# Prologue of an attention and SwiGLU kernel: first loads through one GpSimd queue, key sums on the full array, more TensorE spins

## The chip, the cores and the metric

The kernel runs on one core of one Trainium2 chip (trn2). The metric is device time in microseconds (us) of one execution, the median over runs. Before the change it is 323.82 us, the median of 6 runs (323.05 to 325.52). Engines are named as in the profile: PE is TensorE, DVE is VectorE, ACT is ScalarE, POOL is GpSimd, SP is SyncE. SP and POOL (and ACT, twice at the end) start transfers.

## The reference

Inputs are q, k, v of shape (8, 8, 576, 64) in float32 (batch, heads, sequence, head dimension) and the weights w_gate, w_val (512 x 1536) and w_out (1536 x 512). Two stages follow each other:

```python
q_s = softmax(q, axis=-1)            # over the head dimension
k_s = softmax(k, axis=2)             # over the sequence
kv  = einsum('bhsd,bhse->bhde', k_s, v)
att = einsum('bhsd,bhde->bhse', q_s, kv)
x   = att.transpose(0, 2, 1, 3).reshape(4608, 512)
g   = x @ w_gate
out = (g * sigmoid(g) * (x @ w_val)) @ w_out     # float32, 4608 x 512
```

## The kernel before

Exponentials are taken without subtracting a maximum, and products run in bf16 with float32 sums. A batch has 576 rows, and its eight heads are two groups (G) of four. A group's tile has 128 partitions: partitions 0 to 63 carry one pair of heads (g = 0), 64 to 127 the other (g = 1), and each partition holds T = 9 rows of each head of its pair.

For one group the attention stage is: load q, k and v (`load`, L72, by SP; for batch 0 v is loaded by POOL, cast to bf16 on the way, L358); exp of q and k on ACT (`exp_of`, L119); row sums of exp(q), their reciprocal and the product on DVE (`norm_sum` L132, `norm_mul` L146); nine 128 x 128 transposes of the result on PE, in two PSUM banks of 5 and 4 (`turn_pe` L158, BANKS = (0, 5), (5, 9)), copied out by ACT or DVE (`turn_out` L170); kv, 18 matmuls with 64 contraction rows each; scaling of kv by the reciprocal of the key sums into `kn`; and `x_one` (L213), eight small matmuls whose results are copied into `xt`, the transposed input of the feed-forward stage.

The feed-forward stage works through units. `m_unit` (L278) makes 128 of the 1536 hidden columns for a chunk of tokens: matmuls with the gate weights (`g_ps`) and the value weights (`u_ps`), Silu on ACT (L297), product on DVE (L298). Batch 0 is the first chunk: 12 units, each with 16 matmuls of 320 or 256 columns. `o_unit` (L325) multiplies 128 tokens by w_out and stores. Later chunks interleave `m_unit`, `o_unit` and the attention of the next batch.

The order of instructions on each engine is the order in which the program writes them (`tc.manual_schedule()`), so the body from L344 on sets it. At the start, in before:

- SP issues q group 0 in two pieces, q group 1, k group 0, k group 1 (L345 to L348).
- POOL builds the identity (L343), then issues v group 0, which waits until k group 0 has landed (L360), v group 1, ten weight slices (L361 to L363: 128, 256, 384, 384, 384 columns of w_gate and w_val in turn) and four slices of w_out (L364). The program has eight semaphores for POOL's transfers, so a transfer waits for the eighth before it.
- ACT: exp of q 0 (two pieces), q 1, k 0, k 1, then copies and scalings.
- PE: seven spins that start with the first row sum (`spin`, L377: matmuls of a tile of zeros, whose results nobody reads), the transposes of group 0, `key_sum(0)` (L384: 18 matmuls of k's exp with a column of ones, two row groups of 64), two spins, `key_sum(1)`, one spin, `kv_first(0)` (L400), half the transposes of group 1, `x_one(0, 0)`, the other half, `kv_first(1)`, `x_one(0, 1)`, then `m_unit` 0 to 11.
- SP issues batch 1's loads when the third slice of w_out has landed (L432).

Of the kernel before, what the change touches and what calls it, by code (L numbers as in the profile page):

```python
# [8 lines left out]
FP32 = mybir.dt.float32  # L9
# [6 lines left out]
def kernel(  # L16
# [36 lines left out]
    xt = const.tile([128, KT, n_tok], BF16, name="xt", tag="xt")  # L53
    hr = const.tile([128, MT, RING], BF16, name="hr", tag="hr")
    ident = const.tile([128, 128], BF16, name="ident", tag="ident")
    ones = const.tile([128, 1], BF16, name="ones", tag="ones")
    zero = const.tile([128, 512], BF16, name="zero", tag="zero")
    vbs = [const.tile([128, T, 130], BF16, name=f"vb{i}", tag=f"vb{i}") for i in range(2)]
    v16 = [const.tile([128, 2, T * 64], BF16, name=f"v16_{i}", tag=f"v16_{i}") for i in range(2)]
# [83 lines left out]
        nc.vector.reciprocal(out=rr, in_=rs)  # L143
        return first

    def norm_mul(b, G, pieces=((0, T),)):  # L146
        s = st[b, G]
        eq2 = s["eq"].rearrange("p t h d -> p (t h) d")
        qs = s["qs"] = at.tile([128, T, 128], BF16, tag="qs", name="qs")
        for t0, t1 in pieces:  # L150
            n = 2 * (t1 - t0)
            nc.vector.tensor_mul(  # L152
                qs[:, t0:t1, :].rearrange("p t (h d) -> p (t h) d", d=64),
                eq2[:, 2 * t0:2 * t1, :],
                s["rr"][:, 2 * t0:2 * t1].to_broadcast([128, n, 64]),
            )
# [183 lines left out]

    make_identity(nc, ident)  # L343
    with tc.manual_schedule():  # L344
        load("q", q, 0, 0, BANKS)  # L345
        load("q", q, 0, 1)
        k0 = load("k", k, 0, 0)
        load("k", k, 0, 1)  # L348
        warm = const.tile([128, 1], FP32, name="warm", tag="warm")
        nc.vector.memset(warm, 0.0)  # L350
        nc.scalar.activation(out=warm, in_=warm, func=AF.Exp)
        nc.vector.memset(zero, 0.0)
        nc.vector.memset(ones, 1.0)
        for vb in vbs:
            nc.vector.memset(vb[:, :, 128:129], 1.0)

        for G in range(NG):
            d = nc.gpsimd.dma_start(out=v16[G], in_=head_ap(v, 0, G))  # L358
            if G == 0:
                tc.add_manual_dep(d.ins, k0.ins.name, SYNC, reason="order of loads")  # L360
        for c0, n in ((0, 128), (128, 256), (384, 384), (768, 384), (1152, 384)):  # L361
            w_slice(wg, moe_w_gate, c0, n)
            w_slice(wv, moe_w_val, c0, n)  # L363
        w_dma = [wo_slice(m0, 3) for m0 in (0, 3, 6, 9)]  # L364

        exp_of("q", 0, 0, BANKS)
        exp_of("q", 0, 1)
        exp_of("k", 0, 0)
        exp_of("k", 0, 1)
        first = norm_sum(0, 0, BANKS)  # L370
        norm_mul(0, 0, BANKS)
        norm_sum(0, 1)
        norm_mul(0, 1, BANKS)

        idle = bank("idle")

        def spin(n, after=None):  # L377
            for _ in range(n):
                i = nc.tensor.matmul(out=idle, lhsT=zero[:, 0:128], rhs=zero, start=True, stop=True)  # L379
                if after is not None:  # L380
                    tc.add_manual_dep(i.ins, after.ins.name, SYNC, reason="start of the warm-up")
                    after = None

        def key_sum(G):  # L384
            s = st[0, G]
            s["kv"] = [bank("kv") for _ in range(2)]
            for t in range(T):
                for g in range(2):
                    r = slice(64 * g, 64 * g + 64)
                    nc.tensor.matmul(  # L390
                        out=s["kv"][g][:, 128:129], lhsT=ek_of(0, G, g, t), rhs=ones[r, :],
                        start=(t == 0), stop=(t == T - 1),
                    )
            s["kvr"] = []
            for g in range(2):
                kvr = at.tile([128, 1], FP32, tag=f"kvr{g}", name="kvr")
                nc.vector.reciprocal(out=kvr, in_=s["kv"][g][:, 128:129])
                s["kvr"].append(kvr)

        def kv_first(G):  # L400
            s = st[0, G]
            for t in range(T):
                for g in range(2):
                    r = slice(64 * g, 64 * g + 64)
                    nc.tensor.matmul(
                        out=s["kv"][g][:, 0:128].rearrange("p (h d) -> p h d", d=64),
                        lhsT=ek_of(0, G, g, t), rhs=v16[G][r, :, 64 * t:64 * t + 64],
                        start=(t == 0), stop=(t == T - 1),
                    )
            kn = s["kn"] = at.tile([128, 2, 128], BF16, tag="kn1", name="kn1")  # L410
            nc.scalar.mul(kn[:, 0, :], s["kv"][0][:, 0:128], s["kvr"][0])
            nc.vector.tensor_scalar_mul(kn[:, 1, :], s["kv"][1][:, 0:128], s["kvr"][1])

        spin(7, first)
        turn_pe(0, 0, 0)
        turn_pe(0, 0, 1)
        key_sum(0)
        turn_out(0, 0, 0, nc.scalar)
        turn_out(0, 0, 1, nc.scalar)
        spin(2)  # L420
        key_sum(1)
        spin(1)
        kv_first(0)
        turn_pe(0, 1, 0)
        turn_out(0, 1, 0, nc.scalar)
        x_one(0, 0)
        turn_pe(0, 1, 1)
        turn_out(0, 1, 1, nc.vector)
        kv_first(1)
        x_one(0, 1)  # L430

        load_batch(1, w_dma[-2], by_group=True)  # L432
        load_batch(2)

        for m in range(MT):
            m_unit(0, S, m, by_part=(m == 0))

        for G in range(NG):
            exp_of("q", 1, G)
            exp_of("k", 1, G)  # L440
            cast_v(1, G)
        norm_sum(1, 0)
        norm_mul(1, 0)
        o_unit(0)
        o_unit(1)
        turn_pe(1, 0, 0)
        turn_pe(1, 0, 1)
        turn_out(1, 0, 0, nc.vector)
        turn_out(1, 0, 1, nc.vector)
        kv_one(1, 0)  # L450
        norm_sum(1, 1)
        scale_one(1, 0, (nc.vector, nc.vector))
        norm_mul(1, 1)
        p = o_mm(2)
        x_one(1, 0)
        turn_pe(1, 1, 0)
        turn_pe(1, 1, 1)
        o_out(2, p)
        turn_out(1, 1, 0, nc.vector)
        turn_out(1, 1, 1, nc.vector)  # L460
        kv_one(1, 1)
        scale_one(1, 1, (nc.vector, nc.vector))
        o_unit(3)
        x_one(1, 1)
        for what in ("q", "k"):
            for G in range(NG):
                exp_of(what, 2, G)

        chunks = [(S, 448)] + [(c, 512) for c in range(1024, n_tok, 512)]
        for ci, (c0, n) in enumerate(chunks):  # L470
            b = ci + 2
            jo = 4 * ci
            att = b < B
            final = ci == len(chunks) - 1
            for m in range(MT):
                if ci == 0:
                    if m == 1:
                        cast_v(b, 0)
                        cast_v(b, 1)
                        norm_sum(b, 0)  # L480
                    elif m == 2:
                        norm_mul(b, 0)
                        turn_dma(b, 0)
                    elif m == 3:
                        norm_sum(b, 1)
                    elif m == 4:
                        norm_mul(b, 1)
                        turn_dma(b, 1)
                elif m == 3:
                    if att:  # L490
                        exp_of("q", b, 0)
                        exp_of("q", b, 1)
                        norm_sum(b, 0)
                    o_unit(jo)
                    if att:
                        norm_mul(b, 0)
                        turn_dma(b, 0)
                    o_unit(jo + 1)
                    if att:
                        norm_sum(b, 1)  # L500
                elif m == 4 and att:
                    norm_mul(b, 1)
                    turn_dma(b, 1)
                elif m == 7:
                    if att:
                        exp_of("k", b, 0)
                        exp_of("k", b, 1)
                        cast_v(b, 0)
                        cast_v(b, 1)
                    o_unit(jo + 2)  # L510
                    if not final:
                        o_unit(jo + 3)
                if att and m == 8:
                    kv_both(b)
                    scale_both(b)
                    if b + 1 < B:
                        load_batch(b + 1)
                m_unit(c0, n, m)
                if att and m == 9:
                    x_both(b)  # L520
        o_unit(jo + 3)
        last = n_tok // 128 - 4
        for j in range(last, last + 3):
            o_unit(j)
        o_last(last + 3)
# [30 lines left out]
```

## Time and profile before

| what | value |
|---|---|
| median of 6 runs | 323.82 us |
| the profiled execution | 324.37 us |
| its span in the profile | 322.4 us |
| first load issued (SP) | 0.74 us |
| first exp starts (ACT) | 4.08 us |
| first spin (PE) | 5.73 us |
| first v load issued (POOL) | 9.43 us |
| first kv matmul of group 0 / group 1 | 13.57 / 16.76 us |
| first m_unit starts | 18.97 us |
| first o_unit starts | 43.65 us |

Times in the profile count from the start of its span. A row of the timeline reads: start, duration, engine, line, operation, tile written <- tiles read, shape, number of instructions, and in brackets the idle time before it and what ended that. A row of the chain of waits reads: start, duration, what. The rows of the transfers give the time from issue to landing.

### The profile page before, as it was taken

The numbers are of one execution on the slowest core, as the hardware profiler recorded it, in microseconds if no ns is written. First come the engines' busy times: TensorE is split into PE (matmuls) and PEld (weight loads), VectorE is DVE, ScalarE is ACT, GpSimd is POOL, SyncE is SP. The second block draws the span as 40 slices with busy tenths as digits, with TensorE's granted clock in tenths as the row PEclk, the third lists the DMA queues.
The fourth block names the chain that finished last, engine by engine and source line by source line (L and its number), as shares of the span: only waits on it lengthen the run. The fifth ranks groups of instructions, "written<-read, shape, count | busy, mean of one in ns | idle before, by whom it ended". The sixth has DMA issues, their size and how long they took to land.

```text
span 322.4 us, 4896 instructions
## 1 busy us (share of the span) xinstructions
PE 309.2 (96%) x1902; PEld 153.8 (48%) x1902; DVE 165.5 (51%) x282; ACT 144.3 (45%) x209; POOL 28.8 (9%) x36
## 2 busy tenths in 40 slices
PE   2899998999999999999999999999999999999995
PEld 1468754445444544444444444544444444444443
DVE  4534459388492639354835484457535333333421
ACT  3653363645547355644573467346634122302300
POOL 0850011200110020002000200011000000000000
PEclk9999999999999999999999999999999999999999
DMA  7899999627743944485438633872430112020125
GB/s 239 147 196 204 190 380 393 220 38 201 278 102 69 318 156 103 71 278 196 88 70 249 238 68 72 224 283 47 91 67 0 35 33 65 0 58 9 34 52 115
DMA packets 40360, 45.75 MB, mean 142 GB/s; under 512 B 17424, under 2 KB 24336, under 8 KB 40336
## 3 DMA queue, kind: packets, MB, share of 16 engines
q1 hardware_dynamic: 32752, 39.99, 42.3%
q0 software_dynamic: 7424, 5.31, 11.0%
q8 instruction: 15, 0.25, 0.3%
q10 hardware_dynamic: 160, 0.13, 0.2%
q14 instruction: 9, 0.07, 0.1%
HBM read 37.75 MB, written 9.44 MB: 146 GB/s over the span
## 4 chain that ended last, share of the span: by engine, by line
PE 84%; DMA 6%; DVE 4%; ACT 3%; issue 1%; SPq 0%; POOL 0%
PE g_ps L289 28%; PE u_ps L289 27%; PE o_ps L314 25%; PE kv L191 2%; DMA k<-in_k_dram 2%; DMA out_dram<-o_sb 2%; DMA v<-in_v_dram 2%; DVE rs L138 2%; PE xp L259 1%; ACT eq L124 1%; DVE qs L152 1%; PE o_ps L334 1%; ACT ek L124 1%; DVE hr L298 1%; SPq L77 0%
## 5 line engine op out<-in xcount | busy, mean ns | idle before, releaser
L297 ACT ACTIVATE sg<-g_ps 128x512 bf16<-128x512 f32 (+2 forms) x120 | 65.0, 555 | 138.2 <-PE g_ps L289 132.7
L298 DVE TENSOR_TENSOR hr<-sg,u_ps 128x512 bf16<-128x512 bf16 (+2 forms) x120 | 74.4, 630 | 90.1 <-PE u_ps L289 83.0
L289 PE MATMUL g_ps<-xt,wg 128*128 128x512 bf16 (+2 forms) x480 | 112.4, 361 | 0.3 <-ACT xt L228 0.2
L289 PE MATMUL u_ps<-xt,wv 128*128 128x512 bf16 (+2 forms) x480 | 111.2, 358 | 0.0
L314 PE MATMUL o_ps<-wo,hr 128*128 128x512 bf16 x420 | 93.6, 379 | 0.0
L289 PEld LDWEIGHTS <-wv 128*128 128x128 bf16 x480 | 47.1, 98 | 46.9 <-issue 0.4
L289 PEld LDWEIGHTS <-wg 128*128 128x128 bf16 x480 | 46.2, 99 | 45.9 <-issue 1.3
L314 PEld LDWEIGHTS <-hr 128*128 128x128 bf16 x420 | 41.0, 98 | 49.1
L322 DVE COPY o_sb<-o_ps 128x512 f32<-128x512 f32 x35 | 23.7, 681 | 40.3 <-PE o_ps L314 40.3
L127 POOL CAST vb<-v 128x1152 bf16<-128x1152 f32 x14 | 16.1, 1148 | 176.6 <-DMA v<-in_v_dram 142.7
L138 DVE TENSOR_REDUCE rs<-eq 128x18 f32<-128x1152 bf16 (+2 forms) x17 | 21.6, 1278 | 12.8 <-ACT eq L124 12.8
L152 DVE TENSOR_TENSOR qs<-eq,rr 128x1152 bf16<-128x1152 bf16 (+2 forms) x18 | 21.7, 1214 | 0.1
L124 ACT ACTIVATE eq<-q 128x1152 bf16<-128x1152 f32 (+2 forms) x17 | 18.1, 1104 | 5.1 <-DMA q<-in_q_dram 5.0
L124 ACT ACTIVATE ek<-k 128x1152 bf16<-128x1152 f32 x16 | 18.0, 1158 | 1.0 <-DMA k<-in_k_dram 1.0
L297 ACT ACT_TABLE_LOAD x12 | 15.4, 1283 | 0.2
L124 ACT ACT_TABLE_LOAD x11 | 14.1, 1283 | 0.2
L379 PE MATMUL idle<-zero 128*128 128x512 bf16 x10 | 4.8, 626 | 5.7 <-DVE rs L138 5.7
L191 PE MATMUL kv<-vb,ek 64*128 64x129 bf16 x252 | 8.9, 217 | 0.2 <-DVE hr L298 0.2
L191 PEld LDWEIGHTS <-ek 64*128 64x128 bf16 x252 | 7.4, 94 | 3.0 <-ACT sg L297 2.1
L267 ACT CAST xt<-xp 128x512 bf16<-128x512 f32 x12 | 6.4, 589 | 3.8 <-PE xp L259 3.8
L268 DVE CAST xt<-xp 128x512 bf16<-128x512 f32 x12 | 7.7, 683 | 0.0
L228 ACT CAST xt<-xp 128x320 bf16<-128x320 f32 (+1 forms) x8 | 2.8, 404 | 8.3 <-PE xp L221 8.3
(43 smaller groups left out, 70.5 us busy)
## 6 DMA issues: line engine op xcount, KB each, us to landing
k<-in_k_dram SPq DMA_DIRECT2D x16, 576.0 KB, 7.1
out_dram<-o_sb SPq DMA_DIRECT2D x70, 128.0 KB, 2.4
q<-in_q_dram SPq DMA_DIRECT2D x15, 576.0 KB, 5.1
v<-in_v_dram SPq DMA_DIRECT2D x14, 576.0 KB, 8.9
wo<-in_moe_w_out_dram POOLq DMA_DIRECT2D x4, 384.0 KB, 15.1
wg<-in_moe_w_gate_dram POOLq DMA_DIRECT2D x3, 384.0 KB, 11.3
wv<-in_moe_w_val_dram POOLq DMA_DIRECT2D x3, 384.0 KB, 11.6
v<-in_v_dram POOLq DMA_DIRECT2D x2, 288.0 KB, 5.3
```

The costliest lines, as they stand in the source:

```text
L124: nc.scalar.activation(out=e[:, t0:t1], in_=src[:, t0:t1], func=AF.Exp)
L127: nc.gpsimd.tensor_copy(out=vbs[G][:, :, 0:128].rearrange("p t (h d) -> p t h d", d=64), in_=raw["v", b, G].rearrange("p h (t d) -> p t h ...
L138: i = nc.vector.reduce_sum(out=rs[:, 2 * t0:2 * t1], in_=eq2[:, 2 * t0:2 * t1, :], axis=mybir.AxisListType.X)
L152: nc.vector.tensor_mul(qs[:, t0:t1, :].rearrange("p t (h d) -> p (t h) d", d=64), eq2[:, 2 * t0:2 * t1, :], s["rr"][:, 2 * t0:2 * t1].to_b ...
L191: nc.tensor.matmul(out=kv[g][:, c:c + 129], lhsT=ek_of(b, G, g, t), rhs=vbs[G][r, t, 0:129], start=(t == 0), stop=(t == T - 1),)
L267: nc.scalar.copy(out=xt[:, 2 * G, c0:c0 + 512], in_=main[G][0])
L268: nc.vector.tensor_copy(out=xt[:, 2 * G + 1, c0:c0 + 512], in_=main[G][1])
L289: nc.tensor.matmul(out=ps[i][:, 0:w_], lhsT=w[:, kk, ms], rhs=xt[:, kk, c:c + w_], start=(kk == 0), stop=(kk == KT - 1),)
L297: nc.scalar.activation(out=sg[:, 0:w_], in_=g_ps[:, 0:w_], func=AF.Silu)
L298: nc.vector.tensor_mul(hr[:, m, r:r + w_], sg[:, 0:w_], u_ps[:, 0:w_])
L314: nc.tensor.matmul(out=o_ps, lhsT=hr[:, m, r0:r0 + 128], rhs=wo[:, m, :], start=(m == 0), stop=(m == MT - 1),)
L322: nc.vector.tensor_copy(out=o_sb, in_=o_ps)
```

## The change

All first loads of batch 0 move from SP to POOL and stand in one queue: q 0, q 1, k 0, k 1, v 0, v 1 in two pieces, then the identity, then the weights. v no longer waits for k. q 0 is no longer split. The second half of group 0's q product is made by POOL, ahead of the weights in its queue. The key sums become 9 matmuls per group with all 128 contraction rows and a two-column selector `sel` (column g is one in the partitions of g) in place of 18 with 64 rows. exp of k 1 moves behind group 0's two copies on ACT. Both halves of group 1's transposes move ahead of `key_sum(1)` and `kv_first(0)`. The spins become 8 (from the start) + 6 (with the first row sum) + 3 + 2 + 2 + 2. `kv_first(1)` is written as two pieces, one for each piece of v 1, and the scaling becomes a function of its own. Batch 1's loads wait for the second w_out slice in place of the third.

```diff
-    ones = const.tile([128, 1], BF16, name="ones", tag="ones")
+    sel = const.tile([128, 2], BF16, name="sel", tag="sel")
...
-    def norm_mul(b, G, pieces=((0, T),)):
+    def norm_mul(b, G, pieces=((0, T),), engs=None):
...
-        for t0, t1 in pieces:
+        for (t0, t1), eng in zip(pieces, engs or (nc.vector, nc.vector)):
             n = 2 * (t1 - t0)
-            nc.vector.tensor_mul(
+            eng.tensor_mul(
...
-    make_identity(nc, ident)
     with tc.manual_schedule():
-        load("q", q, 0, 0, BANKS)
-        load("q", q, 0, 1)
-        k0 = load("k", k, 0, 0)
-        load("k", k, 0, 1)
+        for what, src in (("q", q), ("k", k)):
+            for G in range(NG):
+                t_ = raw[what, 0, G] = ld.tile([128, 2, T * 64], FP32, tag=what, name=what)
+                nc.gpsimd.dma_start(out=t_, in_=head_ap(src, 0, G))
+        nc.gpsimd.dma_start(out=v16[0], in_=head_ap(v, 0, 0))
+        for t0, t1 in BANKS:
+            nc.gpsimd.dma_start(out=v16[1][:, :, 64 * t0:64 * t1], in_=head_ap(v, 0, 1, t0, t1))
...
+        nc.vector.memset(sel, 0.0)
+        for g in range(2):
+            nc.vector.memset(sel[64 * g:64 * g + 64, g:g + 1], 1.0)
...
-        for G in range(NG):
-            d = nc.gpsimd.dma_start(out=v16[G], in_=head_ap(v, 0, G))
-            if G == 0:
-                tc.add_manual_dep(d.ins, k0.ins.name, SYNC, reason="order of loads")
+        make_identity(nc, ident)
+
+        exp_of("q", 0, 0, BANKS)
+        exp_of("q", 0, 1)
+        exp_of("k", 0, 0)
+
+        first = norm_sum(0, 0, BANKS)
+        norm_mul(0, 0, BANKS, (nc.vector, nc.gpsimd))
+        norm_sum(0, 1)
+        norm_mul(0, 1, BANKS)
+
         for c0, n in ((0, 128), (128, 256), (384, 384), (768, 384), (1152, 384)):
...
-        exp_of("q", 0, 0, BANKS)
-        exp_of("q", 0, 1)
-        exp_of("k", 0, 0)
-        exp_of("k", 0, 1)
-        first = norm_sum(0, 0, BANKS)
-        norm_mul(0, 0, BANKS)
-        norm_sum(0, 1)
-        norm_mul(0, 1, BANKS)
...
         def key_sum(G):
             s = st[0, G]
-            s["kv"] = [bank("kv") for _ in range(2)]
+            ks = bank("ks")
             for t in range(T):
-                for g in range(2):
-                    r = slice(64 * g, 64 * g + 64)
-                    nc.tensor.matmul(
-                        out=s["kv"][g][:, 128:129], lhsT=ek_of(0, G, g, t), rhs=ones[r, :],
-                        start=(t == 0), stop=(t == T - 1),
-                    )
...
+                nc.tensor.matmul(
+                    out=ks[:, 0:2], lhsT=s["ek"][:, t, :, :].rearrange("p h d -> p (h d)"), rhs=sel,
+                    start=(t == 0), stop=(t == T - 1),
+                )
+            s["kvr"] = at.tile([128, 2], FP32, tag="kvr", name="kvr")
+            nc.vector.reciprocal(out=s["kvr"], in_=ks[:, 0:2])
...
-        spin(7, first)
+        spin(8)
+        spin(6, first)
         turn_pe(0, 0, 0)
         turn_pe(0, 0, 1)
-        key_sum(0)
         turn_out(0, 0, 0, nc.scalar)
         turn_out(0, 0, 1, nc.scalar)
+        exp_of("k", 0, 1)
+        key_sum(0)
+        spin(3)
+        turn_pe(0, 1, 0)
+        turn_pe(0, 1, 1)
+        turn_out(0, 1, 0, nc.scalar)
+        turn_out(0, 1, 1, nc.vector)
+        key_sum(1)
         spin(2)
-        key_sum(1)
-        spin(1)
         kv_first(0)
-        turn_pe(0, 1, 0)
-        turn_out(0, 1, 0, nc.scalar)
+        scale_first(0)
+        spin(2)
         x_one(0, 0)
-        turn_pe(0, 1, 1)
-        turn_out(0, 1, 1, nc.vector)
-        kv_first(1)
+        kv_first(1, *BANKS[0])
+        kv_first(1, *BANKS[1])
+        scale_first(1)
+        spin(2)
         x_one(0, 1)
 
-        load_batch(1, w_dma[-2], by_group=True)
+        load_batch(1, w_dma[-3], by_group=True)
         load_batch(2)
```

More of the change, by code (lines that the diff above doesn't have):

```diff
@@ L352 @@
         nc.vector.memset(zero, 0.0)
-        nc.vector.memset(ones, 1.0)
+        nc.vector.memset(sel, 0.0)
+        for g in range(2):
+            nc.vector.memset(sel[64 * g:64 * g + 64, g:g + 1], 1.0)
         for vb in vbs:
             nc.vector.memset(vb[:, :, 128:129], 1.0)
-        for G in range(NG):
-            d = nc.gpsimd.dma_start(out=v16[G], in_=head_ap(v, 0, G))
-            if G == 0:
-                tc.add_manual_dep(d.ins, k0.ins.name, SYNC, reason="order of loads")
+        make_identity(nc, ident)
[6 more added lines that the diff above has]
+        norm_mul(0, 1, BANKS)
         for c0, n in ((0, 128), (128, 256), (384, 384), (768, 384), (1152, 384)):
@@ L364 @@
         w_dma = [wo_slice(m0, 3) for m0 in (0, 3, 6, 9)]
-        exp_of("q", 0, 0, BANKS)
-        exp_of("q", 0, 1)
-        exp_of("k", 0, 0)
-        exp_of("k", 0, 1)
-        first = norm_sum(0, 0, BANKS)
-        norm_mul(0, 0, BANKS)
-        norm_sum(0, 1)
-        norm_mul(0, 1, BANKS)
-        idle = bank("idle")
         def spin(n, after=None):
+            idle = bank("idle")
             for _ in range(n):
@@ L385, in key_sum, with kv_first @@
             s = st[0, G]
-            s["kv"] = [bank("kv") for _ in range(2)]
+            ks = bank("ks")
             for t in range(T):
-                for g in range(2):
-                    r = slice(64 * g, 64 * g + 64)
-                    nc.tensor.matmul(
-                        out=s["kv"][g][:, 128:129], lhsT=ek_of(0, G, g, t), rhs=ones[r, :],
-                        start=(t == 0), stop=(t == T - 1),
-                    )
[L394 to L400, printed above, removed]
+                nc.tensor.matmul(
[4 more added lines that the diff above has]
+            nc.vector.reciprocal(out=s["kvr"], in_=ks[:, 0:2])
+        def kv_first(G, t0=0, t1=T):
             s = st[0, G]
-            for t in range(T):
+            if t0 == 0:
+                s["kv"] = [bank("kv") for _ in range(2)]
+            for t in range(t0, t1):
                 for g in range(2):
@@ L409, in kv_first, with scale_first @@
                     )
+        def scale_first(G):
+            s = st[0, G]
             kn = s["kn"] = at.tile([128, 2, 128], BF16, tag="kn1", name="kn1")
-            nc.scalar.mul(kn[:, 0, :], s["kv"][0][:, 0:128], s["kvr"][0])
-            nc.vector.tensor_scalar_mul(kn[:, 1, :], s["kv"][1][:, 0:128], s["kvr"][1])
-        spin(7, first)
+            nc.scalar.mul(kn[:, 0, :], s["kv"][0][:, 0:128], s["kvr"][:, 0:1])
+            nc.vector.tensor_scalar_mul(kn[:, 1, :], s["kv"][1][:, 0:128], s["kvr"][:, 1:2])
+        spin(8)
+        spin(6, first)
         turn_pe(0, 0, 0)
         turn_pe(0, 0, 1)
-        key_sum(0)
         turn_out(0, 0, 0, nc.scalar)
         turn_out(0, 0, 1, nc.scalar)
+        exp_of("k", 0, 1)
[6 more added lines that the diff above has]
+        key_sum(1)
         spin(2)
-        key_sum(1)
-        spin(1)
         kv_first(0)
-        turn_pe(0, 1, 0)
-        turn_out(0, 1, 0, nc.scalar)
+        scale_first(0)
+        spin(2)
         x_one(0, 0)
-        turn_pe(0, 1, 1)
-        turn_out(0, 1, 1, nc.vector)
-        kv_first(1)
+        kv_first(1, *BANKS[0])
+        kv_first(1, *BANKS[1])
+        scale_first(1)
+        spin(2)
         x_one(0, 1)
-        load_batch(1, w_dma[-2], by_group=True)
+        load_batch(1, w_dma[-3], by_group=True)
         load_batch(2)
```

## The prediction

> **What bounds the kernel now.** I read the page's busy row first, then the chain of waits for the first 45 us, then the timeline of the same stretch engine by engine, then the landing times of the transfers.
>
> The page's first part:
>
> ```profile
> PE 309.2 (96%) x1902; PEld 153.8 (48%) x1902; DVE 165.5 (51%) x282; ACT 144.3 (45%) x209; POOL 28.8 (9%) x36
> ```
>
> TensorE (PE) is busy 309.2 of 322.4 us. The waits of PE from 60 us to the end sum to 0.4 us. So whatever moves the end of the first feed-forward unit (m_unit 0 of batch 0) moves the end of the program by the same amount, and the change touches only what lies before that point, plus the start of batch 1's loads. The chain of waits (start us, us, what):
>
> ```profile
> 2.28 6.85 DMA k<-in_k_dram
> 9.13 0.30 issue
> 9.43 0.86 POOL v L358
> 10.29 6.43 DMA v<-in_v_dram
> 16.72 0.04 issue
> 16.76 1.16 PE kv L405 x18
> 17.92 0.37 ACT kn L411
> 18.29 0.04 issue
> 18.33 0.71 PE xp L221 x8
> 19.04 2.04 PE g_ps L289 x8
> 21.08 1.18 PE u_ps L289 x8
> 22.25 0.98 PE g_ps L289 x8
> ```
>
> Two things cost time here. First, v is asked for only when k's first load has landed (9.13), so the second v load lands at 16.72. Second, m_unit 0 takes 2.04 + 1.18 = 3.22 us, every later one 0.98 + 0.98 = 1.96: TensorE still runs at half speed. The profile's granted clock says 1.00 throughout, so that column does not show this; the matmul rows do. From the timeline:
>
> ```profile
> 5.73 3.17 PE L379 MATMUL idle<-zero 128*128 128x512 bf16 x7 [5.73 <-DVE rs L138]
> ...
> 10.60 1.16 ACT L124 ACTIVATE ek<-k 128x1152 bf16<-128x1152 f32 x1 [0.28 <-DMA k<-in_k_dram]
> ...
> 13.57 1.14 PE L405 MATMUL kv<-v,ek 64*128 64x128 bf16 x18 [0.82 <-DMA v<-in_v_dram]
> ```
>
> The seven spins start 0.43 us apart (3.0 us in all, transposes follow at 8.69), against about 0.2 us for a 512-column matmul later (o_ps: 24 in 5.34). The 18 kv matmuls take 1.14 us here and 0.70 us in batch 1 (49.69). So the whole start runs slow. From the durations the switch comes inside m_unit 0, near 21.5.
>
> **The change, part by part.** The sum is made against the profiled execution, 324.37 us (span 322.4, 1.97 around it); the median of the six runs, 323.82, is 0.55 lower.
>
> *Loads in one POOL queue.* Removed: five SP loads (0.47 us each to issue) and v's wait for k. Added on POOL: seven issues at the v rows' 0.72 to 0.86 us, 0.74 to about 6.3, then the identity (0.5 us, to 6.9; first needed by the transposes at 8). Landings in before, from the waits on each: q group 0 in halves at 4.05 and 4.7, q1 7.6, k0 9.13, k1 10.57, v0 13.5, v1 16.72. Nothing shows these loads started by POOL at time zero, so I bound them. The first: v0 took 4.1 us from issue to landing, so q0 lands at 0.74 + 4.1 = 4.9, undivided. Here a rule speaks against the change: the Trainium skill, "DMA: Bandwidth & Descriptors", section "Issuing engine by pattern", sends plain loads to SP, and its "Specifications" give a first byte at about 0.6 us there against 1 us by POOL. By the rule q0 would be 0.4 us late, by the rows 0.2 to 0.8; I take the row's 0.8. ACT waits for q1 after that anyway, so it costs nothing at the end. The spacing after it: from below 1.45 us (k0 to k1), from above 3.2 us (v0 to v1). I take 2.4 for the second load, because a newly started stream was slow both times in before (q0 to q1 2.9, v0 to v1 3.2), and 1.5 for the rest, since one queue is not restarted: q1 7.3, k0 8.8, k1 10.3, v0 11.8, v1's parts 12.6 and 13.3. So v1 is 3.4 us earlier, k hardly at all.
>
> *ACT.* eq0 4.9 to 6.2 (1.32), eq1 to 8.5, ek0 8.8 to 10.0 (1.16), then the two qt copies that now stand ahead of ek1 (1.16) to 11.2, ek1 to 12.4. Before it ended at 11.76. This is a new wait, 0.6 us, with key_sum(1) and everything of PE behind it.
>
> *Half of a q multiply on POOL.* No POOL multiply is in the trace. Nearest is the POOL cast, 1148 ns for 1152 elements: 0.5 us for 512 at one input, 1.0 if a second input is read in turn, and 0.8 more if it has to wait for VectorE's half (640 elements, 0.8). So 0.5 to 1.8, and I take 1.0: from rr (7.3) to 8.3, where VectorE alone would need 7.3 + 1.43 = 8.7. Behind it on POOL stand all weight loads, behind it on PE the transposes of group 0, then the qt copies on ACT, which wait for ek0 until 10.0 anyway. Cover: 1.0 us. Even 1.8 stays under it.
>
> *Weights.* Issue from about 8.4, 0.75 each; they sit in the queue behind v1 (13.3) and land from about 14.0 (wg) and 14.8 (wv), then at the rate of before (1.3 us per 256-column slice, 1.93 per 384). m_unit 0 wants the second at 17.5: free by 2.7 us. A slice waits for the load eight before it, which has long landed.
>
> *Key sums.* 2 x 18 matmuls (0.40 us each set) become 2 x 9 full ones with 2 columns: 0.2 at the old 22 ns each, 0.9 at a 98 ns weight load each. I take 0.3; one of them is on the path. Four reciprocals become two, sel's memsets lie in VectorE's idle time before 4.85: nothing.
>
> *Spins.* 10 become 23. The 8 at the start (1.2 to 4.6) run while PE has nothing to do: free. The 6 end at 7.6 fast or 8.9 slow, against transposes ready at 8.1: up to 0.8. The 3 and the first 2 can be on the path, the other pairs lie beside the 0.37 us kn scaling: 0.43 fast, 0.85 slow.
>
> *The path, TensorE fast by 12.4*: key_sum(1) 12.7, spins 13.1, kv_first(0) 0.70 to 13.8, kn with its hand-over 0.5 to 14.3, x_one 0.44 (batch 1's row, 58.64) to 14.7, kv_first(1) 0.70 to 15.4 (v1 landed at 13.3, so no longer a wait), kn to 15.9, x_one to 16.3, xt copies 0.2: m_unit 0 starts at 16.5 and takes 1.96, to 18.5. Before: 22.25. That is -3.7, and the 0.3 to 1.2 us that a later switch costs in this stretch take it to about -3.1.
>
> *The path, TensorE slow until then*: spins to 8.9, transposes 1.17 to 10.1, key sum 10.5, 3 spins 11.8, transposes 13.0, key sum 13.4, spins 14.3, kv 15.4, spins 16.3, x 17.0, kv 18.1, spins 19.0, x 19.7. PE itself is then the bound and starts m_unit 0 at 19.8, against 19.04.
>
> *Which of the two?* The Trainium skill, "TensorE: Matmul & The Clock Gate", Part 1 ("What's actually happening"): the clock doubles after a busy window of about 3.4 us, the windows are not aligned to the program's start, and an idle one takes it back. By the rule, 8 spins (3.4 us), a 1.7 us gap and PE busy without pause from 6.3 on should be fast at 4.5 to 12: -3.1. By the rows it is harder: 5.73 to 9.86 in before was busy for 4.1 us and the spin at 12.14 still took 0.61; 13.57 to 16.5 was nearly full and stayed slow. Nine transposes lie in the one, nine in the other. Only 18.33 to 21.5, plain matmuls without a gap, brought the switch. By the rows, only the kv, spin and x stretch from 13.4 would do it, at 17 to 20: m_unit 0 at about 18.8, fast, to 20.8: -1.5. I lean to the rule, as the 14 first spins are full matmuls and half of their time is new.
>
> *Batch 1's loads* start after the second wo load in place of the third (wo at 33 by the rate above, in before 38.2). They then share the engines with two wo loads: the last, due at 36.9 alone, lands by 40.5 at half rate. PE wants it at 16.5 + 12 x 1.96 + 9 x 0.2 = 41.8. Free by 1.3 us; beyond that a us costs a us. Arriving earlier gains nothing: the exp of batch 1 waits for the last Silu (42.76) and a table load (1.28).
>
> **Rivals.** A, fast TensorE by 12.4 or so: -3.1, 321.3 by the profile, 320.7 by the median; I say 321.0. For it: the length of the spins. Against it: the busy stretches of before that stayed slow.
> B, the spins switch nothing and only the later stretch does: -1.5, 322.6 (322.9 by the profile).
> C, slow until m_unit 0 itself (19.8 + 3.2 less the part already counted, 22.3 to 23): 0 to +0.7, 324.2. The change then doesn't do what it says.
> D, slower: POOL's queue keeps the 3.2 us spacing of v0 to v1 for all six loads. Then v1 lands at 4.9 + 5 x 3.2 = 20.9, m_unit 0 ends 3.7 later (half of kv 0.4, kn 0.5, x 0.5, xt 0.2, the unit 1.96), at 24.6: +2.4, 326.2. It decides from a mean spacing of (22.25 - 3.7 - 4.9) / 5 = 2.7 us. Against it: the weights of this queue land 1.93 us apart at 786 KB read each, more than a q load's 590 KB.
>
> **How the numbers follow.** A 0.52, B 0.23, C 0.12, D 0.13. Measurement can tell about 0.5% (1.6 us) from no change. Faster by more: nearly all of A and a fifth of B, 0.55; within: the rest of B and most of C, 0.29; slower: D and the tail of C, 0.16. Range: down to A with loads 1 us earlier and no lost switch, 319.8; up through B and C, 324.4; D is left out above, and a few hundredths below.
>
> **What would show each step.** q0 near 4.9 and v1's second part near 13.3 on the waits; the 6 spins 0.2 us apart rather than 0.43; 18 kv matmuls in 0.70; m_unit 0 in 1.96 from 16.5; ek1 ending near 12.4; no wait of PE on wo near 40. Wrong if v1 lands after 18.5, if m_unit 0 still takes 3 us, or if POOL's multiply takes over 2 us.

## The result and the profile after

The changed kernel takes 321.63 us (median of 16 runs, 320.74 to 323.69); the kernel before, run beside it, 324.48 (35 runs, 322.86 to 326.14; the 6 runs that the prediction had gave 323.82). The ratio is 0.992, 95% interval 0.9902 to 0.9938: 2.6 us less, clear of the 0.5% that can be told from no change. (Ratios, here and below, leave out executions more than 1.5% above the fastest of the same kernel, one of e2's and two of e11's; medians and ranges keep them.) The profiled execution takes 321.17 us with a span of 319.4, 3.2 less than the profiled one of before.

The chain of waits of the changed kernel (start us, us, what):

```profile
1.27 4.08 DMA q<-in_q_dram
5.35 0.02 issue
5.37 0.75 ACT eq L124
6.12 0.02 issue
6.14 0.83 DVE rs L138
6.97 0.05 issue
7.02 2.74 PE idle L380 x6
9.76 0.96 PE tp L166 x9
...
13.71 0.61 PE kv L403 x18
14.32 0.54 PE idle L380 x2
14.86 0.37 PE xp L221 x8
...
16.77 0.38 PE g_ps L289 x2
17.14 0.02 issue
17.17 0.87 PE g_ps L289 x6
18.04 0.98 PE u_ps L289 x8
19.02 0.98 PE g_ps L289 x8
```

No transfer stands on it after q 0 in this profile; in a second profile of the same kernel (e10, below) k's first load does. m_unit 0 starts at 16.77 (before 19.04; the rows of the timeline begin 0.07 us earlier in both) and takes 2.25 us (before 3.22), so it ends at 19.02 in place of 22.25, 3.23 us earlier: all of the 3.2 us. Where the landings gained can be read in the transfer rates (GB/s moved, 40 slices of 0.5 us from 0 to 20 us); first before, then after:

```profile
GB/s 0 0 0 31 136 289 378 358 356 327 318 180 286 355 383 396 396 267 152 101 9 7 92 166 187 173 154 177 129 86 142 144 179 157 182 184 196 230 185 191
```

```profile
GB/s 0 0 0 0 0 92 147 406 387 396 406 369 194 157 258 341 378 378 406 353 233 210 197 197 197 184 180 178 184 178 196 191 182 198 201 200 206 223 191 198
```

Before has a hole (9 and 7 GB/s, from 10.0 to 11.0) where q and k have been loaded and v has only just been asked for. After starts 1 us later and has none. (v and the weights arrive as bf16, v's load counting 288 KB where q's counts 576, so from there on the figure is half of what is read.)

The timeline of the changed kernel:

```profile
8.01 1.61 POOL L152 TENSOR_TENSOR qs<-eq,rr 128x512 bf16<-128x512 bf16 x1 [0.94 <-DVE rr L143]
...
11.02 1.44 PE L380 MATMUL idle<-zero 128*128 128x512 bf16 x3
...
11.65 1.18 ACT L124 ACTIVATE ek<-k 128x1152 bf16<-128x1152 f32 x1
...
12.25 0.78 PE L166 MATMUL tp<-ident,qs 128*128 128x128 bf16 x9
...
13.65 0.68 PE L403 MATMUL kv<-v,ek 64*128 64x128 bf16 x18
```

TensorE is at half speed in the three spins (three at 0.43 us and the last one's end) and at full speed in kv (0.68, before 1.14): the switch lies near 12.3.

### The profile page after: what moved, and what is told of

Same layout as the page of the kernel before. It is cut to its first block, busy times and chain, and to the rows that moved or that the text cites. A ratio compares the mean times of both kernels' runs of the same rounds, so it can differ in the third digit from the quotient of the medians.

```text
span 319.4 us, 4888 instructions
## 1 busy us (share of the span) xinstructions
PE 310.3 (97%) x1897; PEld 153.3 (48%) x1897; DVE 164.8 (52%) x281; ACT 144.2 (45%) x209; POOL 34.1 (11%) x42
## 3 DMA queue, kind: packets, MB, share of 16 engines
q0 software_dynamic: 8272, 7.67, 13.3%
## 4 chain that ended last, share of the span: by engine, by line
PE 87%; DMA 5%; ACT 3%; DVE 2%; issue 1%; POOLq 0%
PE g_ps L289 28%; PE u_ps L289 27%; PE o_ps L314 25%; DMA q<-in_q_dram 4%; PE kv L191 2%; DMA out_dram<-o_sb 2%; PE idle L380 2%; ACT eq L124 1%; PE xp L259 1%; DVE rs L138 1%; PE o_ps L334 1%; ACT ek L124 1%; DVE hr L298 1%; PE tp L166 0%; DVE qs L152 0%
## 5 line engine op out<-in xcount | busy, mean ns | idle before, releaser
L380 PE MATMUL idle<-zero 128*128 128x512 bf16 x23 | 9.6, 564 | 3.4 <-DVE rs L138 2.2
```

## The experiments

Each ran beside the kernel before on the same chip: e1 to e4 on one chip, e5, e7, e8 and e11 on a second, e9, e10, e12 and e13 on a third. So compare ratios rather than medians between these groups. A difference in us is the ratio's distance from one times that kernel's median.

| kernel | median, us (range) | before, us | ratio (95%) |
|---|---|---|---|
| e1_no_first8 | 321.26 (320.86 to 321.76) | 324.49 | 0.9898 (0.9864 to 0.9931) |
| e2_loads_only | 321.40 (320.57 to 325.69) | 324.49 | 0.9913 (0.9892 to 0.9934) |
| e3_old_loads | 323.29 (322.44 to 324.13) | 324.49 | 0.9965 (0.9951 to 0.9979) |
| e4_first14 | 321.17 (320.85 to 323.17) | 324.49 | 0.9902 (0.9867 to 0.9936) |
| e5_dve_product | 322.15 (321.31 to 322.76) | 324.81 | 0.9924 (0.9895 to 0.9953) |
| e7_no_later_spins | 323.32 (322.04 to 324.89) | 324.81 | 0.9958 (0.9940 to 0.9975) |
| e8_v_no_wait | 327.41 (325.88 to 328.86) | 324.81 | 1.0087 (1.0054 to 1.0120) |
| e11_kv_first | 323.21 (319.83 to 324.95) | 324.81 | 0.9930 (0.9893 to 0.9967) |
| e10_again (the change) | 322.18 (321.16 to 322.45) | 324.44 | 0.9931 (0.9905 to 0.9958) |
| e9_v_after_q1 | 324.53 (321.19 to 325.73) | 324.44 | 0.9980 (0.9958 to 1.0002) |
| e12_kv_first_spins | 320.93 (320.12 to 321.61) | 324.44 | 0.9894 (0.9863 to 0.9925) |
| e13_kv_first_14 | 321.76 (321.21 to 322.67) | 324.44 | 0.9922 (0.9891 to 0.9952) |

**The first spins** (e1).

```diff
-        spin(8)
```

> The changed kernel without its first eight spins; all else stays. Theory (two halves: earlier v loads, and a TensorE that runs fast before m_unit 0, the first spins being needed for the switch): the switch, near 12.3 us in the changed kernel, comes near 15 or later; the transposes of group 1, two spin groups and kv of group 0 run at half speed, +1.0 to +1.5 us against the changed kernel, about 322.9. Rival R1 (the dense work from 7 us on brings the switch, the first spins add nothing): within 0.2 us of the changed kernel, 321.6. Rival R2 (the gain is the clock alone): about 324.

-3.3 us against before, no slower than the whole change (-2.6, intervals overlapping). The theory fell, R1 held for these eight: in this profile the switch comes at about 11, no later than with them. The six spins behind them stand in every version of the change that was run, so whether those are needed is not shown.

**The loads alone** (e2), put into the kernel before.

```diff
-        load("q", q, 0, 0, BANKS)
...
+                nc.gpsimd.dma_start(out=t_, in_=head_ap(src, 0, G))
+        nc.gpsimd.dma_start(out=v16[0], in_=head_ap(v, 0, 0))
+        for t0, t1 in BANKS:
+            nc.gpsimd.dma_start(out=v16[1][:, :, 64 * t0:64 * t1], in_=head_ap(v, 0, 1, t0, t1))
```

> The kernel before with only its first loads changed (one POOL queue, v 1 in two pieces, identity behind them); its spins, key sums, products and PE order stay. Theory: v 1 lands near 13.9 us in place of 16.7, but a slow TensorE in the old order (kv, half the transposes, x, transposes, kv, x) needs until 18.2 to reach m_unit 0 and still runs much of it slow: -0.8 us against before, about 323.7 (with an earlier switch down to 323.0). R1 (the loads bring all of the gain): 321.6. R2 (the clock alone): 324.5, no change.

-2.8 us: all of the gain, R1's number. I had expected a TensorE at half speed. Its timeline:

```profile
7.00 3.17 PE L378 MATMUL idle<-zero 128*128 128x512 bf16 x7 [7.00 <-DVE rs L138]
...
11.52 1.16 ACT L124 ACTIVATE ek<-k 128x1152 bf16<-128x1152 f32 x1 [0.29 <-DMA k<-in_k_dram]
...
13.37 0.68 PE L404 MATMUL kv<-v,ek 64*128 64x128 bf16 x18 [0.25 <-DVE kvr L396]
...
16.74 1.34 PE L289 MATMUL g_ps<-xt,wg 128*128 128x320 bf16 x8
```

With only the old ten spins, kv runs at full speed and m_unit 0 starts at 16.74, as in the changed kernel (16.70). PE no longer waits for v (0.82 us ahead of kv in before): the idle time before kv is 0.25 us, and k 1 (landed at 11.5) is now the late one. The gain is less steady than that of the change: 2 of e2's 20 executions took over 325 us, none of the 24 of the change (16 here, 8 in e10) over 323.7.

**The old loads under the rest of the change** (e3).

```diff
-                nc.gpsimd.dma_start(out=t_, in_=head_ap(src, 0, G))
...
+        load("q", q, 0, 0, BANKS)
+        load("q", q, 0, 1)
+        k0 = load("k", k, 0, 0)
+        load("k", k, 0, 1)
```

> The changed kernel with the old loads (q and k by SP, v by POOL after k 0 has landed); spins, key sums and order as changed. Theory: v 1 lands near 16.7 again; kv of group 1 0.7, scaling 0.5, x 0.45: m_unit 0 starts at 18.4 and runs fast (2.0 to 2.3 us): -1.5 us against before, about 322.9. R1 (all from the loads): 324.5. R2 (the clock alone): 321.6.

-1.1 us, between the theory and R1 and nearer to the theory; m_unit 0 started at 17.87 and took 2.2 us, to 20.0. That end is 2 us earlier than before's, so about a us was lost behind it. The new wait there is for batch 1: its first q load, asked for at 36.76, landed at 42.3, and ACT waited 0.8 us for it.

```profile
42.36 1.28 ACT L124 ACT_TABLE_LOAD   x1 [0.80 <-DMA q<-in_q_dram]
```

The spins and the new order alone do gain, but together with the loads they add nothing measurable to the median: both lead to a TensorE at full speed in m_unit 0, and that can be won only once.

**More first spins** (e4).

```diff
-        spin(8)
+        spin(14)
```

> The changed kernel with 14 spins at the start in place of 8, so that no gap is left before the six. Theory: the switch comes before 8 us in nearly every execution, but key_sum(1) still waits for the second exp of k on ACT (12.8 us), so the median falls by only 0.1 to 0.4 us, to about 321.4, with a narrower spread. Rival (PE at half speed is the bound until 12 us and nothing else is late): 1.0 us less, 320.6. Second rival (more spins stand in the way of the transposes): up to 0.5 us more.

-3.2 us, about what the theory said, but e1 with none was as fast, so the 14 are not what did it. A narrower spread is not shown either (six executions, 320.85 to 323.17).

**The product on VectorE** (e5).

```diff
-        norm_mul(0, 0, BANKS, (nc.vector, nc.gpsimd))
+        norm_mul(0, 0, BANKS, (nc.vector, nc.vector))
```

> The changed kernel with both halves of group 0's q product on VectorE. In the changed kernel POOL's half took 1.61 us and ended at 9.62, where VectorE would end at 9.3; the transposes were held by the six spins until 9.76 and the copies on ACT by exp of k until 10.7. Theory (the half is covered on both sides, and the weights it holds back are early by 2 us): no change, within 0.2 us of the changed kernel, 321.6. Rival (the half on POOL saves time): +0.3 to +0.6. Second rival (it delays the weights): -0.3.

0.9924 against 0.992 of the change: no difference, as expected. Its profile shows something else: here the clock was full from the six spins on and was taken back at 12.16, with all later spins in the program; kv of group 0 took 1.14 us and m_unit 0 started at 17.86 (stretch, length, PE busy and instructions, granted clock, DMA share, GB/s):

```profile
8.75:12.16 3.41, 2.06 (x24) 1.00 1.12 253
12.16:15.57 3.41, 3.41 (x39) 0.50 1.60 188
```

**No later spins** (e7).

```diff
-        spin(3)
...
-        spin(2)
...
-        spin(2)
...
-        spin(2)
```

> The changed kernel without the 3 + 2 + 2 + 2 later spins; the first 8 + 6 stay. Theory R1, which the first runs support (once the loads come early TensorE is dense enough to switch by itself, and the spins ahead of kv stand on the path with 0.45 us): -0.3 to -0.5 us against the changed kernel, about 321.2. Rival (the later spins bring or hold the high clock): m_unit 0 takes 3 us again and the small matmuls run at half speed, +1 to +2.5 us, 322.6 to 324.1.

-1.4 us where the change has -2.6; the rival was right, and R1, which the first four runs had suggested, fell for these nine spins taken together. In e7's chain of waits TensorE gets slow again in the middle, between kv and x:

```profile
13.15 0.65 PE kv L403 x18
13.80 0.37 ACT kn L412
14.17 0.04 issue
14.21 0.70 PE xp L221 x8
14.92 1.12 PE kv L403 x15
...
17.15 2.04 PE g_ps L289 x8
19.19 1.92 PE u_ps L289 x8
```

**v without its wait** (e8), in the kernel before.

```diff
-            if G == 0:
-                tc.add_manual_dep(d.ins, k0.ins.name, SYNC, reason="order of loads")
```

> The kernel before with one line taken out: v's wait for k. POOL then asks for v and the weights from about 1.3 us, beside SP's q and k loads. Theory A (the gain lies in asking for v early; which queue carries it doesn't matter): v is early, q and k share the engines with v and later with weights, k 1 lands near 12; about as the loads of the change alone, 321.4 to 322. Theory B (the order in one queue is what counts): with v and weights beside them q 0 lands 1 us and k 1 some 3 us later, near 14, so that m_unit 0 starts near 18.5: 323.5 to 324.5.

+2.8 us, worse than before: theory B, and beyond its number. v and the weights now run beside q and k. Its transfers (KB each, us from issue to landing):

```profile
k<-in_k_dram SPq DMA_DIRECT2D x2, 576.0 KB, 10.9
...
v<-in_v_dram POOLq DMA_DIRECT2D x2, 288.0 KB, 9.0
q<-in_q_dram SPq DMA_DIRECT2D x1, 576.0 KB, 8.1
```

In before k took 7.3 us. Here exp of q 1 starts at 9.84 (before 7.66), exp of k 1 at 14.35 (before 10.60), and m_unit 0 at 21.57. So early issue alone isn't the gain: v and the weights, asked for early, took their time from k and q. Which of the two, v or the weights, cost more was not tried.

**v after q 1** (e9), in the kernel before.

```diff
-                tc.add_manual_dep(d.ins, k0.ins.name, SYNC, reason="order of loads")
+                tc.add_manual_dep(d.ins, q1.ins.name, SYNC, reason="order of loads")
```

> The kernel before with v waiting for the second q load in place of the first k load; q and k stay on SP. Theory A (the gain is v's earlier landing, and the order in one queue keeps it from costing k): v is asked for 1.5 us earlier, k lands up to 1 us later beside it, v 1 near 15.5: m_unit 0 starts 0.7 to 1.2 us earlier, and with a shorter gap before kv a little more of it runs fast: -0.8 to -1.5 us, about 323.4. Theory B (any v load beside k costs what it gains, as without the wait): 0 to +1 us.

-0.65 us by the ratio, with an interval that reaches 0, and +0.1 by the medians: not enough to decide between A and B. In the profile v was asked for at 8.40 in place of 9.43; beside k's loads v 0 landed at 14.3 (before 13.5) and v 1 near 15.8 (before 16.7). kv of group 0 started at 14.38, after a wait of 1.17 us for v, against 13.57 before, and PE, at half speed from 12 on, could not use the earlier v 1. The profile is of a late execution (325.0): 7 of the 22 took 321.2 to 322.9, less than any of the 29 of before beside them (323.29 at least), and why those were fast is not shown.

**kv ahead of key_sum(1), without later spins** (e11).

```diff
-        key_sum(1)
         kv_first(0)
         scale_first(0)
+        key_sum(1)
         x_one(0, 0)
```

> The kernel without the later spins, and with kv of group 0 and its scaling moved ahead of key_sum(1). In the changed kernel kv of group 0 starts at 13.65, behind key_sum(1), which waits for the second exp of k (12.83); what it needs itself, v 0, has landed by 12.3. Theory (the path to m_unit 0 runs through ACT's exp of k 1 and the spins, not through the clock): kv of group 0 near 12.5, group 1's kv from v 1's landing (13.9), m_unit 0 near 15.9 in place of 16.7: -0.8 us, about 320.8. Rival (v 1 or the clock sets the end): the same as without the later spins, or slower where the clock stays low.

Both happened: the profiled execution, the fastest of the eleven, took 319.83 us, with m_unit 0 at 15.20 and fast, and others up to 324.95. By the medians the gain is 1.6 us, less than the ratio's 2.3. The order can be worth the time; that the late executions lost the clock, as e7's did, is likely but was not profiled.

**The change again (e10), and two versions with both the order and some spins (e12, e13).** e12 is:

```diff
         key_sum(0)
-        spin(3)
+        spin(2)
...
-        key_sum(1)
-        spin(2)
         kv_first(0)
         scale_first(0)
-        spin(2)
+        key_sum(1)
+        spin(1)
```

e13 is e12 with this besides:

```diff
-        spin(8)
+        spin(14)
```

> The changed kernel itself once more, beside the next three on the same chip: -2.6 to -3.0 us against before. A second profile: theory (the moment of the switch depends on where the chip's activity window falls in an execution) puts it at another time than 12.3 us, anywhere from 4.7 to 14, with m_unit 0 starting at 16.4 to 17.2.

> The changed kernel with kv of group 0 ahead of key_sum(1), and the later spins 2 + 1 + 2, each beside a wait of PE (for group 1's product, for kn). Theory (later spins hold the clock across the gaps of 0.4 to 0.6 us; order sets when m_unit 0 starts): m_unit 0 near 15.4 to 15.9, a spread as narrow as the changed kernel's, 320.3 to 320.9. Rival (the spin that was dropped ahead of kv mattered too): a spread to 325 as without the later spins, median 322 to 323.

> The same with 14 first spins, so that TensorE works without a gap from 1.2 us to the six. Theory: the switch comes before 8 us in every execution, the transposes and key sums run fast and the later spins hold it: 320.0 to 320.6, the narrowest spread of all. Rival (the switch at 12 is early enough): as with 8.

The change again gave -2.2 us; in this profile the transposes after the six spins already ran partly fast (9.62, 0.79 us for nine), so the switch lay near 9.6, almost 3 us earlier than in the first profile, and m_unit 0 started at 16.66 all the same. Its chain of waits says why: with a fast TensorE the path runs through k's first load and ACT, where exp of k 1 now stands behind two copies.

```profile
2.86 6.61 DMA k<-in_k_dram
...
9.50 1.16 ACT ek L124
10.66 1.07 ACT qt L111 x2
11.73 1.07 ACT ek L124
```

That exp ends near 12.8 in all three: e2 (12.69), the change (12.83) and e10 (12.80). e12 is the fastest kernel of the study in the median, 1.25 us below the change on the same chip, with m_unit 0 at 16.07 and a narrow spread (320.12 to 321.61), as its theory said; but the intervals of the two ratios overlap (0.9863 to 0.9925, 0.9905 to 0.9958), so the step from the change to e12 is not shown. e13, which should have been the steadiest, is 0.8 slower than e12 in the median, again with overlapping intervals. Its timeline shows what went against the theory:

```profile
7.06 1.47 PE L380 MATMUL idle<-zero 128*128 128x512 bf16 x6 [1.11 <-DVE rs L138]
...
9.71 0.40 PE L166 MATMUL tp<-ident,qs 128*128 128x128 bf16 x4 [0.45 <-POOL qs L152]
...
11.04 0.39 PE L389 MATMUL ks<-sel,ek 128*128 128x2 bf16 x9 [0.94 <-ACT ek L124]
11.29 1.01 PE L380 MATMUL idle<-zero 128*128 128x512 bf16 x2
...
13.20 1.14 PE L403 MATMUL kv<-v,ek 64*128 64x128 bf16 x18
```

The switch did come before 8 us, but it wasn't held: the clock was full at 7.06 and lost again by 11.3, after waits of 0.45 and 0.94 us; kv then ran at half speed.

## Why the prediction came out as it did

**How the clock is given and taken.** The prediction said that the granted clock stays at 1.00 and doesn't show the half speed. That holds for the profiles of before and of the change. In others (e3, e5, e7, e9, e12, e13) the column does show falls to 0.50 and rises from it, and the lengths of the matmuls agree with it there. Such falls and rises lie 3.4 us apart, or a multiple of it: in e7 at 7.44, 10.84, 14.26 and 21.08 (worked out from the share of a slice at 0.50). Cutting e7 there (stretch, length, PE busy and instructions, granted clock, DMA share, GB/s):

```profile
4.03:7.44 3.41, 0.83 (x4) 1.00 0.97 316
7.44:10.84 3.40, 3.21 (x22) 0.50 1.05 331
10.84:14.26 3.42, 2.08 (x48) 1.00 1.50 186
14.26:17.67 3.41, 2.95 (x37) 0.50 1.41 180
17.67:21.08 3.41, 3.41 (x16) 0.50 1.30 200
```

And e12, at its own moments:

```profile
7.46:10.88 3.42, 2.82 (x14) 0.50 1.03 344
10.88:14.29 3.41, 2.90 (x52) 1.00 1.47 191
14.29:17.70 3.41, 3.39 (x48) 1.00 1.49 195
```

The rows fit together if each decides the clock of the next. The Trainium skill, "TensorE: Matmul & The Clock Gate", Part 1, has windows of this length that aren't aligned to the program; the rows agree (3.41). It also says that an idle window takes the clock back; here a window that was busy for 2.08 of 3.42 us did (e7), and one with 2.90 didn't (e12, the same stretch with three spins in it). In the other direction 2.82 us with spins in it gave it (e12), 2.95 us of kv, x and 0.5 us of m_unit 0 didn't (e7), nor did 3.04 us of kv, transposes and x (e9, 15.38 to 18.79). Busy time alone doesn't sort these windows. Full matmuls, such as the spins, seem to count for more than transposes and than kv and x, which use part of the array (64*128 and 64*64 in their rows). That is read from a few windows and wasn't tried by itself. e9, on the old order, went the same way: full speed by 8.6, taken back near 12 after its wait for k (1.57 us), and given again only at 22.2, inside m_unit 0.

**Point by point.**

- *What bounds the kernel*: right for the change. The end of m_unit 0 moved by 3.23 us and the span by 3.0. It isn't a rule: in e3 a us of the gain was lost to batch 1's loads.
- *POOL's queue*: the first issue was at 1.27, not 0.74. q 0 landed 4.1 us after it, as taken from v, hence at 5.35. q 1 came at 7.8 (7.3 taken), k 0 at 9.5 (8.8), k 1 at 11.0 (10.3), v 0 at 12.3 (11.8), v 1 at 13.9 (13.3). The term was 0.5 to 0.7 us too small, nearly all of it the late issue; the spacings were as taken. For v it didn't reach the end, since PE's kv of group 1 came at 15.16. For k it is close: in e10, with a faster TensorE, k 0 is on the chain.
- *The rule that plain loads belong on SP* (the Trainium skill, "DMA: Bandwidth & Descriptors", "Issuing engine by pattern"): q 0 was indeed 0.65 us later (5.35 against 4.7), as the rows had it rather than the rule's 0.4. It heads the chain, but key_sum(0), to which that chain leads, waited for exp of k 0 until 10.70 in any case. e2 gained 2.8 us against the rule, yet the same order with q and k on SP was not run, so the rule itself is not refuted. Rival D fell: the mean spacing was (13.9 - 5.35) / 5 = 1.7 us, under 2.7. (Its parts sum to 3.56 us, not 3.7, which would make the bound 2.8.)
- *ACT*: exp of k 1 ended at 12.83 (12.4 taken), just as PE reached key_sum(1) at 13.03. The new wait exists, level with PE's own work in the first profile and on the chain in e10, where PE waited 0.58 us for it. In e11 and e12, which take it off the path, m_unit 0 starts 1.5 and 0.6 us earlier, but both also have fewer spins.
- *The POOL product*: 1.61 us against 1.0 taken and 1.8 at most. It began beside VectorE's half (0.82 us), so 0.8 of waiting and 0.8 of work would fit; no run separates them. Covered, as said (e5).
- *Key sums*: 0.3 us was taken; nine full matmuls took 0.40 at half and 0.38 at full speed, as long as the 18 smaller ones (0.40 in before, 0.38 in e2). They save nothing here.
- *Weights and batch 1*: no wait of PE on either; SP asked for batch 1 at 34.1 in place of 38.3, and o_unit 0 wasn't held.
- *Spins*: the 8 are free, and no gain of theirs is to be seen (e1). The 6 ran at half speed and stand on the chain with 2.74 us; they held the first five transposes, ready at 8.71, until 9.76. That costs little, as key_sum(0) behind them waits for exp of k 0 until 10.70 in any case.
- *The path*: 16.5 + 1.96 was forecast for full speed by 12.4, plus some loss for a late switch: -3.1 by the profile. It was 16.77 + 2.25: -3.2. The 0.3 us in m_unit 0 fits a wait for xt of group 1, whose first copy on DVE ends at 17.15, just ahead of the third matmul (17.17). So of the 0.6 us set aside for a late switch the start took 0.3, and 0.3 went to something else.
- *Which of the two*: the switch came near 12.3 as in case A, but the moment is luck: in e10, the same program, it came near 9.6. Nor was the reason right. I named the 14 first spins; e1 and e4 show that 0, 8 or 14 ahead of the six make no difference (the six were never left out), and e7 that the later ones do, though e5 shows that they don't always hold the clock. And I added two gains, early v and a fast TensorE, where the loads alone bring both (e2). That this is so because the wait for v is gone, and with it a gap in which TensorE idles, is argued and not shown.

The 0.6 us between the forecast 321.0 and 321.63 is the base: before's median moved from 323.82 to 324.48. In sum the loads' part of the gain was foreseen. The spins' part was not as forecast, since the loads alone gain as much, and the fit of the number owes something to luck.

*Left open*: whether q and k on SP with v behind them in one order would do as well, since v is cast in its transfer and stays on POOL, and so whether the one queue or the mere order brings the gain of e2; what the key sums, the transposes' new place and batch 1's earlier request are worth, none of which was taken out alone; and what decides, from one execution to the next, whether the clock holds. Why the change with everything isn't faster than its loads alone is answered in part: the end of exp of k 1 is the same in both, and m_unit 0 starts about 4 us after it.

## What to carry to other kernels

Where the start of a program is bound by transfers, put the loads into one queue in the order in which they are needed, with no wait between them: asking early for v and the weights in a second queue cost 2.8 us here, the same loads in order gained 2.8. Spins helped here in the short waits just ahead of the work that has to be fast (e7 without them gains 1.2 us less), not at the start (e1, e4): in e13 what was won early was lost again over waits of half a microsecond to one. They don't make the clock sure (e5). Read more than one profile of a kernel whose clock moves: the chain of waits of the same program went through TensorE's spins in one and through k's load and ACT in the other. And gains that lead to the same state, here a TensorE at full speed in the first unit, don't add.

## What was not expected of the hardware

TensorE lost its full clock in stretches in which it was busy for 2.08 of 3.42 us (e7), 2.06 of 3.41 (e5) and 1.74 of 3.41 (e13), and didn't regain it in one with 2.95 of 3.41, of kv and x for the most part. POOL could first issue a transfer at 1.27 us, while SP did at 0.74.
